# The last of three chained products as seven half-size block products per pair of token tiles

## The chip, the cores and the metric

One core of one Trainium2 chip runs the whole program. The metric is the device time of one execution in microseconds (us). TensorE (PE) multiplies, VectorE (DVE) and ScalarE (ACT) do the elementwise work, GpSimd (POOL) small steps, and the SyncE queue (SP) issues the transfers, DMA transposes among them.

## The reference, cut to what matters

```python
def _attn_ref(q, k, v, g_norm):                     # 4 batches, 8 heads, 576 tokens, 64 wide
    kv = np.einsum('bhsd,bhse->bhde', k, v)
    out = np.einsum('bhsd,bhde->bhse', q, kv)
    rms = np.sqrt(np.mean(out * out, axis=-1, keepdims=True) + 1e-06)
    return out / rms * g_norm                       # -> x: 2304 tokens x 512

def _moe_ref(x, w_in, w_out):                       # 512 -> 2048 -> 512
    h = x @ w_in
    sp = np.where(h > 20.0, h, np.log1p(np.exp(np.minimum(h, 20.0))))
    return (h * np.tanh(sp)) @ w_out

def _moe2_ref(x, w_in, w_out, g_ln):                # 512 -> 1024 -> 512
    h = x @ w_in
    e = np.exp(h - np.max(h, axis=-1, keepdims=True))
    solu = h * (e / (np.sum(e, axis=-1, keepdims=True) + 1e-09))
    mu = np.mean(solu, axis=-1, keepdims=True)
    var = np.mean((solu - mu) ** 2, axis=-1, keepdims=True)
    return ((solu - mu) / np.sqrt(var + 1e-06) * g_ln) @ w_out     # the last product
```

The weights arrive as 64-bit floats.

## The kernel before, in words

**Number form.** A value that goes into a large product is kept as two fp16 parts, a high one (a rounding, by ACT) and a low one (the rest, by DVE), and a product of two such values is three matmuls (`PASS`: high*high, high*low, low*high), added up in PSUM.

**First mixture.** The 2304 tokens are six blocks of 384 (b = 0 to 5), the 2048 hidden columns four groups of 512 (g). PE runs 24 units H(b, g) (lines 595 to 606: four times 12 matmuls of 384 columns) and 24 units Y(b, g) (lines 631 to 646: the same number), H ahead of Y, so that the Y units of the last block are over last. `w1` and `w2` hold the weights of the two products, `g` (three buffers) the activations between them. The staging tiles `st` (five) and `P` (five) serve to decode the weights: ACT scales (`sc`), POOL takes signs (`sg`), DVE joins the bits (`low`, `put`), ACT makes the high part (`whi`), DVE the low one (`wlo`). The pieces of the second mixture's weights, `w3` (8) and `w4` (8), go the same way, late in the first mixture, into a pool of their own (`w34`).

**Second mixture.** It goes by 18 token tiles t of 128. H2(t) (lines 709 to 726) is 24 matmuls of 512 columns into one of two two-bank PSUM tiles. Then comes the row work: the row's maximum on DVE (`mx`), the exponential on ACT (`ex`), the product `z` on DVE, its sum of squares on ACT (`sq2`), small steps on DVE and POOL (`inv`, `var`, `pw`), the normalisation on DVE (`ln`), the high part on ACT (`hi`), the low part on DVE (`lo`), one DMA transpose from `hl` into `lnT` (`T`, line 790). O(t) (lines 794 to 805) is 24 matmuls of 512 columns into one PSUM bank: 8 slices of the 1024 inputs, times three passes, 128 tokens by all 512 output columns. ACT scales the bank into `osb` (`oc`, line 809) and SP writes it out (`out`, line 812). H2(t) needs `z` of tile t-2, since that frees its PSUM tile.

**Order.** The program first collects tasks with an engine, a cost, what they come after and, for PE, a due time from a nominal sequence (`pe`, lines 222 to 226, and `nominal`). A list planner (`Plan.order`) then lays them out per engine: at each engine the one that is ready and due first. `Plan.search` moves due times of tasks of the first 160 us at random, 300 times, and keeps what does not lengthen the plan's end. What comes out is one fixed order per engine; at run time each engine goes through its queue and waits on semaphores. Where the plan leaves PE a gap in the first 150 us, `keep_warm` (line 1066) puts idle matmuls of 256 columns there.

Of the kernel before, what the change touches and what calls it, by code (L numbers as in the profile page):

```python
# [8 lines left out]
FP32 = mybir.dt.float32  # L9
# [131 lines left out]
def tile_attn_moe_moe2(  # L141
# [52 lines left out]
    psA = psA_cm.__enter__()  # L194


    st_p = ctx.enter_context(pool("stage", NST, side="right"))
    dec_p = ctx.enter_context(pool("dec", NDEC, side="right"))
    g_p = ctx.enter_context(pool("g", NG, side="right"))
# [21 lines left out]
    hs, ys = iter(units), iter(units)  # L221
    pe = [("H", *next(hs)) if x == "H" else ("Y", *next(ys)) for x in line]
    pe += [("2", 0), ("2", 1)] + [("Y", *u) for u in ys] + [("2", 2)]
    for t in range(3, NT2):
        pe += [("O", t - 3), ("2", t)] if t < NT2 - 1 else [("2", t)]
    pe += [("O", t) for t in range(NT2 - 4, NT2)]
    MM = 0.1625
    nominal, at_ = {}, 26.0
    for u in pe:
        nominal[u] = at_  # L230
        at_ += 48 * MM if u[0] in "HY" else 24 * 0.216

# [258 lines left out]
    W_in, W_out, W2_in, W2_out = (words(x) for x in (w_in, w_out, w2_in, w2_out))  # L491

    def w1_item(f):
        s = slice(f * 128, (f + 1) * 128)
# [22 lines left out]
    def w4_item(kk):  # L517
        def load(t):
            nc.sync.dma_start(out=t, in_=W2_out[kk * 128:(kk + 1) * 128, :])
        return (load, (lambda: (w34["w4"][:, kk, 0], w34["w4"][:, kk, 1])),  # L520
                gl[:, kk:kk + 1], 1)
# [5 lines left out]
    PIECES += [("3", j) for j in range(8)] + [("4", j) for j in range(8)]  # L527
    ITEM = {"1": w1_item, "2": w2_item, "3": w3_item, "4": w4_item}
    items = {u: ITEM[u[0]](u[1]) for u in PIECES}
    piece = {}  # L530

    def w_load(u):
        t = st_p.tile([128, 1024], I32, tag="st", name="st")
        items[u][0](t)
        piece[u] = [t, None]

# [69 lines left out]

# [7 lines left out]

    def g_hi(b, grp, i):
        if i == 0:
            g_t[b, grp] = g_p.tile([128, 2, G, BLK], FP16, tag="g", name="g")
# [66 lines left out]
    def open_w34():  # L684
        at_cm.__exit__(None, None, None)
        w34_cm.append(pool("w34", 1, side="right"))
        p = w34_cm[0].__enter__()
        w34["w3"] = p.tile([128, C, 2, F2], FP16, name="w3")
        w34["w4"] = p.tile([128, K2, 2, DM], FP16, name="w4")


    ph2 = {}
# [87 lines left out]
    def s_hi(t):  # L780
        hl = T[t, "hl"] = ph2["p"].tile([128, 2, F2], FP16, tag="hl", name="hl")
        nc.scalar.activation(out=hl[:, 0], in_=T[t, "z"], func=ACTF.Copy)  # L782

    def s_lo(t):
        hl = T[t, "hl"]
        nc.vector.tensor_tensor(out=hl[:, 1], in0=T[t, "z"], in1=hl[:, 0], op=ALU.subtract)  # L786

    def s_T(t):
        lnT = T[t, "lnT"] = st_p.tile([128, 2 * K2, 128], FP16, tag="st", name="lnT")
        nc.sync.dma_start_transpose(out=lnT, in_=T[t, "hl"].rearrange("p a f -> p (a f)"))  # L790

    outv = out.rearrange("(b p r) c -> b r p c", p=128, r=R)

    def emit_O(t):
        lnT = T[t, "lnT"]
        w4 = w34["w4"]
        op = T[t, "op"] = psY.tile([128, 512], FP32, tag=f"y{t % 4}", name="op")
        m = 0
        for kk in range(K2):
            for la, wa in PASS:  # L800
                nc.tensor.matmul(  # L801
                    out=op, lhsT=lnT[:, K2 * la + kk], rhs=w4[:, kk, wa],
                    start=(m == 0), stop=(m == 3 * K2 - 1),
                )
                m += 1

    def o_copy(t):
        osb = T[t, "osb"] = dec_p.tile([128, DM], FP32, tag="P", name="osb")
        nc.scalar.activation(out=osb, in_=T[t, "op"], func=ACTF.Copy, scale=2.0 ** -16)

    def o_out(t):
        nc.sync.dma_start(out=outv[t // R, t % R], in_=T[t, "osb"])


    def task(key, engine, cost, fn, args, after=(), lag=0.1, due=None):
# [170 lines left out]
    for n, (b, grp) in enumerate(units):  # L986
# [16 lines left out]
        if last:  # L1003
# [17 lines left out]
                    last_of[c] = [("ylo", b, c)]  # L1021


    task(("open2",), "-", 0.0, open_2, (),
         [("glo", *u, i) for u in units for i in range(2)]
         + [("ylo", b, c) for b in range(NI) for c in range(C)] + [("open",)], 0.0)
    for t in range(NT2):
        y = [("ylo", t // R, c) for c in range(C)]
        w = [("wlo", ("3", j)) for j in range(8)]
        task(("2", t), "P", 5.2, emit_H2, (t,),  # L1030
             [("open2",)] + y + w + ([("z", t - 2), ("2", t - 1)] if t > 1 else []), 0.25,
             nominal["2", t])
# [11 lines left out]
        stb = ("put", PIECES[len(PIECES) - NST + t]) if t < NST else ("O", t - NST)  # L1044
        task(("T", t), "S", 1.4, s_T, (t,), [("lo", t), stb], 2.6)
        w = [("wlo", ("4", j)) for j in range(8)]
        bank = last_of[t] if t < 4 else [("oc", t - 4)]
        task(("O", t), "P", 5.2, emit_O, (t,),
             [("T", t), ("O", t - 1) if t else None] + w + bank, 0.25, nominal["O", t])
        decb = ("wlo", PIECES[len(PIECES) - NDEC + t]) if t < NDEC else ("out", t - NDEC)  # L1050
        task(("oc", t), "A", 0.58, o_copy, (t,), [("O", t), decb])
        task(("out", t), "S", 0.9, o_out, (t,), [("oc", t)], LAND)


    nc.scalar.preload_act_table_set("mish")
# [83 lines left out]
```

## Time and profile before

| what | value |
|---|---|
| median of 3 runs | 626.46 us |
| all runs | 626.46, 749.81, 624.45 us |
| span of the profiled execution | 624.8 us |
| PE busy share of the span | 99% |
| matmuls of the last product | 432 of 512 columns |

The span runs from the first to the last instruction of the one profiled execution. It lies between the two lower runs and 1.7 us below the median. Busy time of PE is not PE at its peak, since matmuls overlap; what one matmul costs in a stream is the distance from start to start.

### The profile page before, as it was taken

The page shows a single profiled execution, that of the slowest core. Times are in us where ns is not written, and L with a number is a line of the kernel's source. Part 1 is how long each engine was busy: PE and PEld are TensorE (multiplying, and loading weights), DVE is VectorE, ACT ScalarE, POOL GpSimd, SP SyncE. Part 2 cuts the span into 40 slices and gives each one's busy share as a digit, 9 for nine tenths or more (in the row PEclk, how much of TensorE's full clock was granted, in tenths as well). Part 3 has the DMA queues.
Part 4 walks back from the last instruction along what each step waited for, and adds up shares of the span by engine and source line. Part 5 has one row for each costly group of instructions (what it writes and reads, how often), then busy time and mean ns, then how long its engine had stood idle before and what let it go on. Part 6 is the DMA issues. An engine that isn't in the chain of part 4 may idle for free.

```text
span 624.8 us, 9988 instructions
## 1 busy us (share of the span) xinstructions
PE 616.5 (99%) x4103; PEld 353.7 (57%) x4103; DVE 310.9 (50%) x534; ACT 267.3 (43%) x459; POOL 95.5 (15%) x126
## 2 busy tenths in 40 slices
PE   8999999999999999999999999999999999999997
PEld 6766666666666666566666666654445444444443
DVE  1688788882113531333122288937777245555410
ACT  3668557663313423332333266616444233343311
POOL 1534632210000210013001143200010000000000
PEclk9899999999999999999999999999999999999999
DMA  8999685852022250014000254201430533343331
GB/s 295 300 255 209 186 175 169 268 99 64 1 77 77 57 121 1 0 35 69 17 2 18 76 211 169 102 1 34 69 67 5 120 78 76 76 79 74 80 106 50
DMA packets 97965, 61.99 MB, mean 99 GB/s; under 512 B 72064, under 2 KB 89472, under 8 KB 97920
## 3 DMA queue, kind: packets, MB, share of 16 engines
q1 hardware_dynamic: 97760, 61.36, 38.7%
q8 instruction: 32, 0.52, 0.4%
q14 instruction: 13, 0.11, 0.1%
q10 hardware_dynamic: 160, 0.00, 0.0%
HBM read 39.33 MB, written 4.72 MB: 70 GB/s over the span
## 4 chain that ended last, share of the span: by engine, by line
PE 92%; DMA 5%; ACT 2%; SPq 0%; DVE 0%; issue 0%; ACTq 0%
PE y L641 30%; PE hp L601 28%; PE op L801 15%; PE h L718 15%; DMA qraw<-in_q_dram 2%; DMA st<-in_moe_w_in_dram 2%; PE kvp L294 2%; PE xo L432 1%; DMA xT<-xhl 1%; DMA yT<-in_k_dram 1%; ACT P L542 0%; PE rT L370 0%; ACT qhl L406 0%; ACT xhl L468 0%; ACT g L618 0%; ACT m L611 0%
## 5 line engine op out<-in xcount | busy, mean ns | idle before, releaser
L641 PE MATMUL y<-g,w 128*128 128x384 f16 x1152 | 201.3, 326 | 0.0
L601 PE MATMUL hp<-xT,w 128*128 128x384 f16 x960 | 166.7, 327 | 0.8 <-DMA xT<-xhl 0.5
L601 PEld LDWEIGHTS <-w 128*128 128x128 f16 x1152 | 111.8, 98 | 75.2 <-issue 1.3
L641 PEld LDWEIGHTS <-w 128*128 128x128 f16 x1152 | 111.8, 98 | 74.4
L718 PE MATMUL h<-w,yT 128*128 128x512 f16 x432 | 96.0, 379 | 0.0
L801 PE MATMUL op<-w,lnT 128*128 128x512 f16 x432 | 95.2, 379 | 0.0
L623 DVE SCALAR_TENSOR_TENSOR g<-m,g 128x768 f16<-128x768 f32 x48 | 46.3, 970 | 95.6 <-ACT g L618 95.5
L611 ACT ACTIVATE m<-hp 128x384 f32<-128x384 f32 x96 | 46.2, 488 | 107.3 <-PE hp L601 106.4
L801 PEld LDWEIGHTS <-lnT 128*128 128x128 f16 x432 | 42.3, 98 | 50.7
L718 PEld LDWEIGHTS <-yT 128*128 128x128 f16 x432 | 42.3, 98 | 50.1
L547 POOL TENSOR_SCALAR st<-st 128x512 f32<-128x512 f32 x48 | 43.6, 918 | 101.5 <-ACT P L542 98.0
L618 ACT ACTIVATE g<-m 128x768 f16<-128x768 f32 x48 | 39.9, 838 | 26.2 <-PE y L641 25.7
L552 DVE SCALAR_TENSOR_TENSOR st<-st 128x512 int32<-128x512 int32 x48 | 36.6, 780 | 11.2 <-POOL st L547 11.2
L735 ACT ACTIVATE e<-h,nb 128x1024 f32<-128x1024 f32 x18 | 20.1, 1116 | 51.4 <-DVE nb L730 30.2
L542 ACT ACTIVATE P<-st 128x512 f32<-128x512 f32 x48 | 31.7, 669 | 15.8 <-DMA st<-in_moe_w_out_dram 7.9
L452 POOL TENSOR_SCALAR ms<-ms 128x8 f32<-128x8 f32 x15 | 5.4, 363 | 210.4 <-DVE ms L447 210.1
L559 DVE SCALAR_TENSOR_TENSOR P<-P,st 128x512 int32<-128x512 int32 x48 | 34.5, 745 | 0.1
L601 PE MATMUL hp<-yT,w 128*128 128x384 f16 x192 | 33.3, 326 | 0.0
L729 DVE TENSOR_REDUCE mx<-h 128x1 f32<-128x1024 f32 x18 | 22.0, 1224 | 20.5 <-PE h L718 20.5
L768 POOL TENSOR_SCALAR var<-var 128x1 f32<-128x1 f32 x18 | 3.4, 190 | 178.9 <-DVE var L763 178.9
L742 DVE SCALAR_TENSOR_TENSOR z<-h,e 128x1024 f32<-128x1024 f32 x18 | 22.0, 1224 | 17.5 <-ACT e L735 17.5
L786 DVE TENSOR_TENSOR hl<-z,hl 128x1024 f16<-128x1024 f32 x18 | 22.0, 1224 | 14.9 <-ACT hl L782 14.9
(95 smaller groups left out, 438.8 us busy)
## 6 DMA issues: line engine op xcount, KB each, us to landing
st<-in_moe_w_in_dram SPq DMA_DIRECT2D x24, 512.0 KB, 5.4
st<-in_moe_w_out_dram SPq DMA_DIRECT2D x24, 512.0 KB, 4.4
yT<-in_k_dram SPq DMA_DIRECT2D x16, 288.0 KB, 5.4
yT<-in_v_dram SPq DMA_DIRECT2D x16, 288.0 KB, 5.6
out_dram<-osb SPq DMA_DIRECT2D x18, 256.0 KB, 2.8
qraw<-in_q_dram SPq DMA_DIRECT2D x3, 768.0 KB, 6.3
qraw<-in_q_dram SPq DMA_DIRECT2D x4, 384.0 KB, 8.2
qraw<-in_q_dram SPq DMA_DIRECT2D x4, 192.0 KB, 5.2
```

The source lines that it names most:

```text
L542: nc.scalar.activation(out=P, in_=v[:, :, 1], func=ACTF.Copy, scale=2.0 ** -111)
L547: nc.gpsimd.tensor_scalar(out=v[:, :, 1], in0=v[:, :, 1], scalar1=0.0, scalar2=1.0, op0=ALU.mult, op1=ALU.mult)
L552: nc.vector.scalar_tensor_tensor(out=v[:, :, 0], in0=v[:, :, 0], scalar=29, in1=v[:, :, 1], op0=ALU.logical_shift_right, op1=ALU.bitwise_or)
L559: nc.vector.scalar_tensor_tensor(out=P.bitcast(I32), in0=P.bitcast(I32), scalar=3, in1=v[:, :, 0], op0=ALU.logical_shift_left, op1=ALU.bit ...
L601: nc.tensor.matmul(out=h_t[b, grp, i], lhsT=w1[:, c, wa, f:f + 128], rhs=xT_t[b][:, C * xa + c], start=(c == 0 and m == 0), stop=(c == C - ...
L611: nc.scalar.activation(out=m_t[b, grp, i // 2][:, i % 2], in_=h_t.pop((b, grp, i)), func=ACTF.Mish, scale=2.0 ** -16)
L618: nc.scalar.activation(out=g_t[b, grp][:, 0, 2 * i:2 * i + 2], in_=m_t[b, grp, i], func=ACTF.Copy, scale=64.0)
L623: nc.vector.scalar_tensor_tensor(out=g_t[b, grp][:, 1, j], in0=m_t.pop((b, grp, i)), scalar=64.0, in1=g_t[b, grp][:, 0, j], op0=ALU.mult, ...
L641: nc.tensor.matmul(out=y_t[cc][:, 0:BLK], lhsT=w2[:, grp * G + ii, wa, cc * 128:(cc + 1) * 128], rhs=g_t[b, grp][:, ga, ii], start=(first ...
L718: nc.tensor.matmul(out=hp[:, half], lhsT=y[:, c, ya, tok], rhs=w3[:, c, wa, half * 512:(half + 1) * 512], start=(m == 0), stop=(m == 3 * C ...
L729: nc.vector.reduce_max(out=mx, in_=T[t, "hp"], axis=AX.X)
L801: nc.tensor.matmul(out=op, lhsT=lnT[:, K2 * la + kk], rhs=w4[:, kk, wa], start=(m == 0), stop=(m == 3 * K2 - 1),)
```

## The change

The tiles are taken in nine pairs. The pair's 256 rows of normalised `z` are a 2x2 block matrix, tile by half of the 1024 inputs, and the weight `w4` is a 2x2 block matrix, half of the inputs by half of the 512 output columns. O(p) for pair p is seven block products in Strassen's manner (Winograd's sums), each 4 slices x 3 passes = 12 matmuls of 256 columns, in the order 1, 2, 6, 7, 5, 4, 3. They need four sums of row blocks per pair (`s_sum`) and four sums of weight blocks, once (`w4_sums`). Products 6, 5, 3 go on top of product 1 in one PSUM bank (A), product 4 on top of 7 in another (D), product 2 stands alone (B). Between the additions intermediate states are taken out: `e1` (after 1), `e2` (after 6) and `e7` (after 7) by ACT into `part_e`, `c11`, `c22`, `c21` by DVE and `c12` by ACT into the output rows.

Places: the seven weight blocks lie in the first 14 of 16 column blocks of `w1` (whose layout is now by column block), the transposed rows (two buffers) in `w2`, `part_e` in the ends of both, and the rows before the transpose (`HL`, two buffers) over all the staging tiles `st` and over all of `g`. So these wait for the last reads of what lay there.

```diff
-    w1 = big.tile([128, C, 2, F1], FP16, name="w1")
+    w1 = big.tile([128, F1 // 128, C, 2, 128], FP16, name="w1")
...
-    for t in range(3, NT2):
-        pe += [("O", t - 3), ("2", t)] if t < NT2 - 1 else [("2", t)]
-    pe += [("O", t) for t in range(NT2 - 4, NT2)]
+    pe += [("2", 3)]
+    for p in range(2, NT2 // 2):
+        pe += [("2", 2 * p), ("2", 2 * p + 1), ("O", p - 2)]
+    pe += [("O", p) for p in range(NT2 // 2 - 2, NT2 // 2)]
...
+    w4 = w1f[:, 0:56 * HB].rearrange("p (k a q n) -> p k a q n", k=4, a=2, q=7)
+    lnTs = [w2f[:, 7168 * i:7168 * i + 7168].rearrange("p (c t) -> p c t", t=128) for i in range(2)]
...
+    def w4_scale(u):
+        P = piece[u][1]
+        nc.scalar.activation(out=P, in_=P, func=ACTF.Copy, scale=items[u][2])
+    def w4_sums(j):
+        a, b, t = piece["4", j][1], piece["4", j + 4][1], w34["t4"]
+        lo, hi = slice(0, HB), slice(HB, 2 * HB)
+        for o, x, y in ((t[:, 0], a[:, hi], a[:, lo]), (t[:, 1], b[:, hi], t[:, 0]),
+                        (t[:, 2], b[:, hi], a[:, hi]), (t[:, 3], b[:, lo], t[:, 1])):
+            nc.vector.tensor_tensor(out=o, in0=x, in1=y, op=ALU.subtract)
...
+    HL = [st_all.rearrange("p n w -> p (n w)").bitcast(FP16), g_all.rearrange("p n a i t -> p (n a i t)")]
+    SUMS = ((4, 2, 3, ALU.add), (5, 4, 0, ALU.subtract), (6, 0, 2, ALU.subtract),
+            (7, 1, 5, ALU.subtract))
+    PART = {"a": (0, 2, 0), "b": (3, 6, 2), "c": (6, 8, 5)}
+    def s_sum(p):
+        Q = T[p, "Q"]
+        for o, x, y, op in SUMS:
+            nc.vector.tensor_tensor(out=Q[:, o], in0=Q[:, x], in1=Q[:, y], op=op)
...
+    PROD = {1: (0, 0, "A", True), 2: (1, 1, "B", True), 6: (4, 4, "A", False),
+            7: (5, 5, "D", True), 5: (3, 3, "A", False), 4: (2, 6, "D", False),
+            3: (6, 2, "A", False)}
+    ORDER = (1, 2, 6, 7, 5, 4, 3)
+    def emit_O(p, i):
+        x, w, bank, first = PROD[i]
...
+        for kk in range(4):
             for la, wa in PASS:
                 nc.tensor.matmul(
-                    out=op, lhsT=lnT[:, K2 * la + kk], rhs=w4[:, kk, wa],
+                    out=T[p, bank][:, 0:HB], lhsT=lnTs[p % 2][:, 8 * x + 4 * la + kk],
+                    rhs=w4[:, kk, wa, w], start=(first and m == 0),
...
-        task(("hi", t), "A", 1.05, s_hi, (t,), [("ln", t)] + ([("T", t - 2)] if t > 1 else []))
-        task(("lo", t), "V", 1.23, s_lo, (t,), [("hi", t)])
-        task(("T", t), "S", 1.4, s_T, (t,), [("lo", t), stb], 2.6)
-        task(("oc", t), "A", 0.58, o_copy, (t,), [("O", t), decb])
...
+        if p > 1:
+            before = [("T", p - 2, x) for x in "abc"]
+        elif p:
+            before = [("Yd", *u) for u in units[-NG:]]
+        else:
+            before = [("put", u) for u in PIECES[-NST:]]
+        task(("sum", p), "V", 2.8, s_sum, (p,), lns)
...
+        for x, c in (("a", 1.4), ("b", 2.1), ("c", 1.4)):
+            buf = [("O", p - 2, i) for i in ORDER] if p > 1 else [("Yd", *u) for u in (units[-4:] if p else units[-4:-2])]
+            task(("T", p, x), "S", c, s_T, (p, x), [("lo", p, x)] + buf, 2.6)
+        where = {1: "a", 2: "a", 6: "b", 7: "c", 5: "b", 4: "b", 3: "c"}
+            needs = {6: [("e1", p)], 5: [("e2", p)], 4: [("e7", p)], 3: [("c22", p)]}.get(i, [])
...
+        task(("e1", p), "A", 0.38, o_keep, (p, 0, "A"), [("O", p, 1)] + old + gate)
+        task(("e2", p), "A", 0.38, o_keep, (p, 1, "A"), [("O", p, 6)] + old + gate)
+        task(("e7", p), "A", 0.38, o_keep, (p, 2, "D"), [("O", p, 7)] + old + gate)
+        task(("c11", p), "V", 0.42, o_add, (p, 0, 0, "B", 0), [("O", p, 2), ("e1", p)] + slots + decb)
+        task(("c22", p), "V", 0.42, o_add, (p, 1, 1, "A", 2), [("O", p, 5), ("e7", p)] + slots + decb)
+        task(("c21", p), "V", 0.42, o_add, (p, 1, 0, "D", 1), [("O", p, 4), ("e2", p), ("c22", p)])
+        task(("c12", p), "A", 0.38, o_copy, (p,), [("O", p, 3), ("c11", p)])
```

Part "a" of a pair is its first tile (two blocks), "b" three blocks (the second tile's second half and two sums), "c" the other two sums; each has its own `hi`, `lo` and transpose. The pair's `z` blocks and sums lie in `Q`, two buffers. The weight part for slice j (`w4t`, `w4hr`, `w4ht`, `w4lr`, `w4lt`) waits for the units H(5, ·) that read the column blocks of `w1` that it overwrites.

## Rows read from the trace of the kernel before

**Rows 1.** The page: busy time by engine, granted clock in 40 slices, the chain by engine and line
```profile
PE 616.5 (99%) x4103; PEld 353.7 (57%) x4103; DVE 310.9 (50%) x534; ACT 267.3 (43%) x459; POOL 95.5 (15%) x126
PEclk9899999999999999999999999999999999999999
PE 92%; DMA 5%; ACT 2%; SPq 0%; DVE 0%; issue 0%; ACTq 0%
```

**Rows 2.** Windows (start:end, length; busy us and count per engine; clock, DMA share, GB/s)
```profile
0.00:60.00 60.00, 55.35 (x671) 40.47 (x671) 36.57 (x69) 36.35 (x70) 22.80 (x31) 0.97 1.01 264
360.00:420.50 60.50, 60.50 (x366) 35.62 (x364) 44.97 (x60) 33.54 (x59) 15.76 (x16) 1.00 0.34 120
420.50:585.00 164.50, 164.50 (x793) 77.50 (x792) 94.42 (x208) 67.56 (x101) 12.59 (x34) 1.00 0.34 69
440.00:480.00 40.00, 40.00 (x205) 19.83 (x203) 31.11 (x69) 19.05 (x30) 3.69 (x10) 1.00 0.29 51
564.28:585.00 20.72, 20.72 (x98) 9.41 (x96) 11.04 (x24) 7.97 (x12) 1.48 (x4) 1.00 0.35 77
585.00:624.80 39.80, 36.26 (x169) 16.23 (x166) 5.52 (x12) 7.57 (x12) 0.74 (x2) 1.00 0.27 73
```

**Rows 3.** Timeline of PE and weight loads (start us, length, line, shape, count, idle before)
```profile
47.35 3.33 PE L1068 MATMUL hp<-ident 128*128 128x256 f16 x29
47.35 3.04 PEld L1068 LDWEIGHTS <-ident 128*128 128x128 f16 x28
...
409.27 2.11 PE L601 MATMUL hp<-xT,w 128*128 128x384 f16 x12
...
489.65 2.11 PE L641 MATMUL y<-g,w 128*128 128x384 f16 x12
...
574.48 5.34 PE L801 MATMUL op<-w,lnT 128*128 128x512 f16 x24
...
584.84 36.42 PE L801 MATMUL op<-w,lnT 128*128 128x512 f16 x168
```

**Rows 4.** Groups by shape (count; busy us, mean ns of one), second mixture
```profile
L801 PEld LDWEIGHTS <-lnT 128*128 128x128 f16 x432 | 42.3, 98 | 50.7
L786 DVE TENSOR_TENSOR hl<-z,hl 128x1024 f16<-128x1024 f32 x18 | 22.0, 1224 | 14.9 <-ACT hl L782 14.9
L782 ACT ACTIVATE hl<-z 128x1024 f16<-128x1024 f32 x18 | 19.0, 1053 | 21.5 <-DVE z L777 17.6 <-DMA lnT<-hl 3.8
L809 ACT ACTIVATE osb<-op 128x512 f32<-128x512 f32 x18 | 10.6, 588 | 30.6 <-PE op L801 30.5
```

**Rows 5.** Groups by shape up to 420 us: nearest forms to the new instructions
```profile
L459 DVE SCALAR_TENSOR_TENSOR xf<-xo,rho 128x512 f32<-128x512 f32 x15 | 10.4, 691 | 19.9 <-POOL rho L454 19.9
L579 DVE SCALAR_TENSOR_TENSOR w<-P,gl,w 128x512 f16<-128x512 f32 x8 | 5.6, 741 | 0.1
L677 DVE SCALAR_TENSOR_TENSOR yT<-y,yT 128x384 f16<-128x384 f32 x8 | 4.5, 556 | 11.9 <-ACT yT L669 11.8
L311 DVE SCALAR_TENSOR_TENSOR kvr<-kvp,kvr 64x256 f16<-64x256 f32 x6 | 2.5, 419 | 0.3 <-ACT kvr L305 0.2
L611 ACT ACTIVATE m<-hp 128x384 f32<-128x384 f32 x96 | 46.2, 488 | 107.3 <-PE hp L601 106.4 <-DVE g L623 0.6
```

**Rows 6.** Transfers of the second mixture: size, count, us from issue to landing
```profile
out_dram<-osb SPq DMA_DIRECT2D x18, 256.0 KB, 2.8
lnT<-hl SPq DMA_TRANSPOSE x18, 4.3
```

**Rows 7.** Timeline: first row maximum, the last tile's transpose issue, first and last output copies
```profile
420.50 1.23 DVE L729 TENSOR_REDUCE mx<-h 128x1 f32<-128x1024 f32 x1 [6.73 <-PE h L718]
...
590.22 0.60 ACT L809 ACTIVATE osb<-op 128x512 f32<-128x512 f32 x1 [2.44 <-PE op L801]
...
596.61 1.83 SPq L790 DMA_TRANSPOSE lnT<-hl  x1
...
621.35 0.60 ACT L809 ACTIVATE osb<-op 128x512 f32<-128x512 f32 x1 [4.58 <-PE op L801]
```

More of the change, by code (lines that the diff above doesn't have):

```diff
@@ L194, in tile_attn_moe_moe2 @@
     psA = psA_cm.__enter__()
-    st_p = ctx.enter_context(pool("stage", NST, side="right"))
+    st_p = ctx.enter_context(pool("stage", 1, side="right"))
+    st_all = st_p.tile([128, NST, 1024], I32, name="st")
     dec_p = ctx.enter_context(pool("dec", NDEC, side="right"))
-    g_p = ctx.enter_context(pool("g", NG, side="right"))
+    g_p = ctx.enter_context(pool("g", 1, side="right"))
+    g_all = g_p.tile([128, NG, 2, G, BLK], FP16, name="g")
     at_cm = pool("attn", 1, side="right")
@@ L519, in load @@
             nc.sync.dma_start(out=t, in_=W2_out[kk * 128:(kk + 1) * 128, :])
-        return (load, (lambda: (w34["w4"][:, kk, 0], w34["w4"][:, kk, 1])),
-                gl[:, kk:kk + 1], 1)
+        return load, None, gl[:, kk:kk + 1], 1
     w34 = {}
@@ L616, in g_hi @@
         if i == 0:
-            g_t[b, grp] = g_p.tile([128, 2, G, BLK], FP16, tag="g", name="g")
+            g_t[b, grp] = g_all[:, units.index((b, grp)) % NG]
         nc.scalar.activation(
@@ L792, in tile_attn_moe_moe2 @@
-    outv = out.rearrange("(b p r) c -> b r p c", p=128, r=R)
[L794 to L797, printed above, removed]
+    HL = [st_all.rearrange("p n w -> p (n w)").bitcast(FP16), g_all.rearrange("p n a i t -> p (n a i t)")]
+    HL = [x[:, 0:14 * 512].rearrange("p (q a f) -> p q a f", q=7, a=2) for x in HL]
+    SUMS = ((4, 2, 3, ALU.add), (5, 4, 0, ALU.subtract), (6, 0, 2, ALU.subtract),
+            (7, 1, 5, ALU.subtract))
@@ L798, in emit_O @@
+    ORDER = (1, 2, 6, 7, 5, 4, 3)
+    def emit_O(p, i):
+        x, w, bank, first = PROD[i]
+        if first:
+            n = (3 * p + "ABD".index(bank)) % 4
+            T[p, bank] = psY.tile([128, 512], FP32, tag=f"y{n}", name="op")
         m = 0
-        for kk in range(K2):
+        for kk in range(4):
             for la, wa in PASS:
                 nc.tensor.matmul(
-                    out=op, lhsT=lnT[:, K2 * la + kk], rhs=w4[:, kk, wa],
-                    start=(m == 0), stop=(m == 3 * K2 - 1),
+                    out=T[p, bank][:, 0:HB], lhsT=lnTs[p % 2][:, 8 * x + 4 * la + kk],
+                    rhs=w4[:, kk, wa, w], start=(first and m == 0),
+                    stop=(m == 11), skip_group_check=not first,
@@ L804, in emit_O, with o_keep @@
                 )
                 m += 1
[L807 to L812, printed above, removed]
+    OUT = 2.0 ** -16
+    def o_keep(p, n, bank):
+        e = T[p, "e", n] = part_e[p % 2][:, n]
+        nc.scalar.activation(out=e, in_=T[p, bank][:, 0:HB], func=ACTF.Copy, scale=OUT)
@@ new lines, in osb, with o_add, o_copy @@
+    def osb(p, t):
+        if (p, "osb", t) not in T:
+            T[p, "osb", t] = dec_p.tile([128, DM], FP32, tag="P", name="osb")
+        return T[p, "osb", t]
+    def o_add(p, t, half, bank, n):
+        nc.vector.scalar_tensor_tensor(
+            out=osb(p, t)[:, half * HB:half * HB + HB], in0=T[p, bank][:, 0:HB], scalar=OUT,
+            in1=T[p, "e", n], op0=ALU.mult, op1=ALU.add)
+    def o_copy(p):
+        nc.scalar.activation(
+            out=osb(p, 0)[:, HB:2 * HB], in_=T[p, "A"][:, 0:HB], func=ACTF.Copy, scale=OUT)
@@ L1050, in tile_attn_moe_moe2 @@
-        decb = ("wlo", PIECES[len(PIECES) - NDEC + t]) if t < NDEC else ("out", t - NDEC)
-        task(("oc", t), "A", 0.58, o_copy, (t,), [("O", t), decb])
-        task(("out", t), "S", 0.9, o_out, (t,), [("oc", t)], LAND)
+    for p in range(NT2 // 2):
+        if p > 1:
[4 more added lines that the diff above has]
+            before = [("put", u) for u in PIECES[-NST:]]
+        lns = [("ln", 2 * p), ("ln", 2 * p + 1)]
+        task(("hi", p, "a"), "A", 1.05, s_hi, (p, "a"), lns[:1] + before)
+        task(("lo", p, "a"), "V", 1.23, s_lo, (p, "a"), [("hi", p, "a")])
+        task(("sum", p), "V", 2.8, s_sum, (p,), lns)
+        for x, c in (("b", 1.45), ("c", 1.05)):
+            task(("hi", p, x), "A", c, s_hi, (p, x), [("sum", p)] + before)
+            task(("lo", p, x), "V", c + 0.2, s_lo, (p, x), [("hi", p, x)])
+        for x, c in (("a", 1.4), ("b", 2.1), ("c", 1.4)):
+            buf = [("O", p - 2, i) for i in ORDER] if p > 1 else [("Yd", *u) for u in (units[-4:] if p else units[-4:-2])]
+            task(("T", p, x), "S", c, s_T, (p, x), [("lo", p, x)] + buf, 2.6)
+        w = [("wlo", ("4", j)) for j in range(4)]
+        where = {1: "a", 2: "a", 6: "b", 7: "c", 5: "b", 4: "b", 3: "c"}
+        bank = {i: (3 * p + n) % 4 for i, n in ((1, 0), (2, 1), (7, 2))}
+        prev = ("O", p - 1, 3) if p else None
+        for i in ORDER:
+            needs = {6: [("e1", p)], 5: [("e2", p)], 4: [("e7", p)], 3: [("c22", p)]}.get(i, [])
+            if i in bank:
+                n = bank[i]
+                needs = list(free_y.get(n, last_of[n])) if p else list(last_of[n])
+            task(("O", p, i), "P", 1.32, emit_O, (p, i), [("T", p, where[i])] + w + needs,
+                 0.25, nominal["O", p] + 1.32 * ORDER.index(i))
+            if prev:
+                plan.line([prev, ("O", p, i)])
+            prev = ("O", p, i)
+        old = [("c11", p - 2), ("c22", p - 2), ("c21", p - 2)] if p > 1 else []
+        gate = [("H", NB - 1, 3, i) for i in range(G)] if p == 0 else [("Yd", *units[-1])] if p == 1 else []
+        decb = ([("wlo", u) for u in PIECES[-NDEC:]] if p < 3 else [])
+        slots = [("out", p - 2, 0), ("out", p - 2, 1)] if p > 1 else []
+        task(("e1", p), "A", 0.38, o_keep, (p, 0, "A"), [("O", p, 1)] + old + gate)
[5 more added lines that the diff above has]
+        task(("c12", p), "A", 0.38, o_copy, (p,), [("O", p, 3), ("c11", p)])
+        task(("out", p, 0), "S", 0.9, o_out, (p, 0), [("c11", p), ("c12", p)], LAND)
+        task(("out", p, 1), "S", 0.9, o_out, (p, 1), [("c21", p), ("c22", p)], LAND)
+        free_y[(3 * p) % 4] = [("c12", p)]
+        free_y[(3 * p + 1) % 4] = [("c11", p)]
+        free_y[(3 * p + 2) % 4] = [("c21", p)]
```

91 lines of the change are left out of this document (66 added, 25 removed).

## The prediction

> **What bounds it now.** I read the page first: PE is busy for 99% of the span, the chain that ended last is PE for 92%, and the granted clock stands at 9 tenths of full speed or more in all but the second of the 40 slices [rows 1], that is at the upper of its two levels. So a microsecond comes off only where PE issues fewer or shorter matmuls, and anything that makes PE wait is added in full. The windows say where PE did idle: 4.65 us in the first 60 us, and after its last matmul; from 360 us to 585 us it was busy throughout [rows 2]. DVE has most to do of the others: 74% of 360 to 420.5 us, 57% of 420.5 to 585 us, 78% of 440 to 480 us, where units of Y lay between the H2 tiles (the last 12 matmuls of Y begin at 489.65) [rows 2, 3]. PE still idled nowhere there, so 78% is a DVE load that this order is known to bear. The timeline gives the price of a matmul in a stream, from start to start: 168 of 512 columns in 36.42 us make (36.42 - 0.379)/167 = 0.2158 us each, 12 of 384 columns (2.11 - 0.326)/11 = 0.162 [rows 3].
>
> **The last product.** Removed: per pair 48 matmuls of 512 columns, 48 x 0.2158 = 10.36 us. Added: 7 x 12 = 84 of 256 columns. None such is in the last product before, but the idle matmuls of `keep_warm` have just this shape, each with a weight load: 29 in 3.33 us, (3.33 - 0.273)/28 = 0.1092 us [rows 3]; a straight line through 384 and 512 columns gives 0.1086. I take 0.1092: 84 x 0.1092 = 9.17 us. The gain is 1.19 us per pair, 10.7 us for nine (11.1 at 0.1086). That is 1.7%, and no other term of PE shrinks, so 624.8 - 10.7 = 614.1 us is the floor but for what the search may find in the first 60 us.
>
> Weight loads rise from 432 to 756, 98 ns each [rows 4], and now sit under matmuls of 109 ns. The idle stream shows 28 such loads in the same 3.33 us [rows 3], so they are hidden, with 11 ns to spare. The Trainium skill (TensorE: Matmul & The Clock Gate, section on packing small matmuls, The mechanism) says that a weight load overlaps matmuls in flight only where their row groups differ, which speaks against this change: all 128 rows are used here, and a pair would cost 84 x (0.109 + 0.098) = 17.4 us by it. The trace does not bear that out, at 256 columns or at 384.
>
> **Waits within a product.** Product 6 waits for `e1`, 5 for `e2`, 4 for `e7` (ACT), 3 for `c22` (DVE); between what they wait for and them lies one other product, 12 x 0.1092 = 1.31 us. An ACT copy of 256 columns out of PSUM is 0.39 us (from 488 ns at 384 and 588 at 512), a DVE addition 0.42 (419 for 64x256; 556 at 384 is its upper end) [rows 4, 5]; the chain moves from PE to the output copy within 0.1 us (the first of the seven tiles ends about 590.2, the copy starts at 590.22) [rows 3, 7]. That leaves 0.85 us. Behind `e1` on ACT are queued the exponentials and squares, behind `c22` the maxima and `z`; PE waits if the engine stands in something longer, or in something that is itself late. On DVE those are the maxima and `lo` at 1.22 (4 per pair), the three-block `lo` at 1.76, and the four sums, 4 x 0.69 = 2.76 if together. At a random moment this costs ((1.22 - 0.85)^2/2 x 4 + 0.91^2/2 + 1.91^2/2)/19.53 = 0.13 us for `c22`; the ACT waits a tenth of it each. That is 1.5 us over nine pairs. The order is fixed in advance and every lag shifts it, so I take 4 us, 0.11 us for each of the 36 waits; the ends are 0 and 18 (0.5 us each).
>
> **DVE and ACT.** A pair of tiles now takes DVE 11.04 us of 20.72 [rows 2]. The change adds the sums (2.76; 691 ns each from a DVE instruction of two inputs and 512 columns [rows 5]), a `lo` of 1536 columns (1.224 + 512 x 1.044 ns = 1.76; the slope is from 556 at 384 to 1224 at 1024 [rows 4, 5]) beside the two of 1024 that stay, and three additions (1.26): 16.82 us. PE needs 2 x 5.18 + 9.17 = 19.53 us, so DVE stands at 86%. ACT goes from 7.97 to 7.97 - 1.18 + 1.45 + 1.56 = 9.80 us, 50%. DVE stays below PE, and H2 can run well ahead of O (two buffers each of `Q`, `HL` and `lnT`), so its lag is bridged, until the last pair. Over the stage DVE has 94.42 + 5.52 us [rows 2] plus 9 x 5.78 = 152 us. It starts at 420.5 [rows 7]; its last `lo` must be over when the transpose (4.3 us [rows 6]) and the last four products (5.24 us) still fit before PE's end, 621.3 - 10.7 = 610.6: by 601. That is 152 of 180.5 us, 84%.
>
> **Weights.** `w4` costs DVE 8 x 0.741 = 5.9 us now [rows 5]. After: 16 subtractions of 256 columns (6.7) and low parts 4 x (0.42 + 0.69 + 1.22) = 9.3, so 10.1 us more; ACT has 8 x 0.59 + 4 x (0.39 + 0.59 + 1.05) = 12.8 where about 8 x 0.59 = 4.7 were, 8 more. In 360 to 420.5 us DVE goes from 45.0 to 55.1 of 60.5 us, ACT from 33.5 to 42 [rows 2]. The cover is the 6.73 us in which DVE waits for the first maximum [rows 7] and the last three units of Y, 3 x 48 x 0.162 = 23 us of PE, that come before O(0). I cost it at nothing; without the cover up to 10 us go into the DVE stage above, which then needs 90%. The waits for old places (`w1`, `w2`, `st`, `g`) end with H(5, ·), the last `put` and the last Y. The strictest is pair 1, whose rows lie over `g` and wait for all of Y; while they wait PE has Y itself and H2. Nothing.
>
> **Transposes.** Three per pair where there were two, with 1.75 times the columns, on SP's queue, each behind O of two pairs before. A DMA share of 0.35 [rows 2] becomes at most 0.61. Hidden, but at the end. There the last transpose was issued 11.6 us after the last H2 (585.0 to 596.61 [rows 2, 7]); the sums and the longer `hi` and `lo` add 2.76 + 0.4 + 0.54, and the landing takes 4.3 to 6.5 us (three blocks for two), so product 6 of the last pair can start 19.6 to 21.8 us after the last H2. If two pairs and two products are left for PE then, that is 2 x 9.17 + 2.62 = 20.96 us of work. Before, seven tiles were left (36.42 us [rows 3]), so I expect three pairs or more, and charge 1 us; with one pair left it would be 9.
>
> **The sum.** 624.8 - 10.7 + 4 + 1 = 619.1. The span lies between the shown runs, 1.7 us below their median; I say 619.
>
> **Rivals.** About 2% is what a measurement of this kernel can tell from no change, so between 613.9 and 639 us (612.3 and 637.3 on the scale of the span) it is called the same.
>
> First, the waits within a product take the gain. At 10.7/36 = 0.30 us for each of the 36 the gain is gone (624.8), at (637.3 - 614.1)/36 = 0.64 it is over 2% slower; at 0.5 it gives 614.1 + 18 = 632. For it: a DVE at 86% and a fixed order; PE has no other ready work when H2 in turn waits for `z`. Against: 0.85 us of slack at each, and ACT half idle.
>
> Second, the one on the other side: DVE becomes the bound, in the stage after 420.5 us. The 180.5 us above grow by as much as the end is late, so it decides from where DVE can be kept busy for no more than 79% of the time (152/(180.5 + 10.7): no gain) and 75% (152/(180.5 + 23.2): over 2% slower). With 80% and 5 us of weights left over, 157/0.8 = 196 us, 15.7 late: 630. For it: nothing in the trace shows more than 78% in this stage. Against: that was what was asked of it, not its limit; with H2 ahead there is nearly always another tile's step ready.
>
> Third, it doesn't do what it says: 256 columns cost more than 0.1092 us in this stream, where operands and weights change at every matmul, unlike in the idle one. At 10.36/84 = 0.1233 the gain is gone; with loads wholly exposed, 756 x 0.098 = 74 us more, 688. The skill's rule above would give that. The hidden loads at 384 and 256 columns speak against it: a chance of 0.03, 0.01 of it for the loads wholly exposed.
>
> Fourth, over 2% faster: nearly no waits, and up to 4.65 us of PE's idle time in the first 60 us [rows 2] gone, as the search runs anew and keeps other moves. 609.5 at best. It can as well lose some.
>
> **Chances.** Forecast 0.68 (its own range 614 to 624), waits 0.13, DVE 0.11, matmul price 0.03, faster 0.05. Over 2% slower: a third of the waits' case, under a half of DVE's, most of the third: 0.12. Faster 0.05, the rest 0.83. The range leaves out the faster case and the upper halves of the first two rivals with the third, under 0.2: 613 to 632.
>
> **What would show it.** Right: products of 12 matmuls 1.31 us apart, PE without gaps over 0.2 us in O, DVE at 80 to 90% from 430 to 590 us, three or more pairs after the last H2. Wrong: PE idle before products 6, 5, 4 released by ACT, or before 3 by DVE (first rival); PE idle before H2, released by `z`, or one long gap in the last pair behind a transpose (second); a stream of 256 columns over 0.115 us (third); idle time before 415 us that was not there, if the weights' cover fails.

## The result, and the profile after

The changed kernel takes 617.5 us (616.5 to 618.0) where the kernel before takes 625.66 us: a ratio of 0.9873, interval 0.9857 to 0.989. One of the four runs behind the 625.66 was slow (749.81 us); the ratio is that of the fast runs. Forecast were 619 us and 613 to 632. The profiled execution has a span of 614.5 us and a time of 616.5 us; before, the span was 624.8 us.

The page of the changed kernel, the same parts as in [rows 1]:

```profile
PE 602.5 (98%) x4427; PEld 382.7 (62%) x4427; DVE 365.0 (59%) x626; ACT 289.5 (47%) x498; POOL 95.9 (16%) x126
PEclk9999999999999999999999999999999999999999
PE 90%; DMA 6%; ACT 2%; issue 1%; DVE 1%; POOL 0%; SPq 0%; POOLq 0%; ACTq 0%
```

PE is still what the time hangs on: it lost 14 us of busy time, while DVE gained 54 and ACT 22.

PE's timeline (start us, length, shape, count, idle time before and what ended it). L861 is the last product, L753 is H2, L676 is Y:

```profile
474.93 2.11 PE L676 MATMUL y<-g,w 128*128 128x384 f16 x12
476.88 5.40 PE L861 MATMUL op<-w,w 128*128 128x256 f16 x48
482.67 5.40 PE L861 MATMUL op<-w,w 128*128 128x256 f16 x48 [0.39 <-DVE osb L880]
489.12 5.41 PE L861 MATMUL op<-w,w 128*128 128x256 f16 x48 [1.04 <-DMA w<-g]
494.37 5.34 PE L753 MATMUL h<-w,yT 128*128 128x512 f16 x24
499.55 1.47 PE L861 MATMUL op<-w,w 128*128 128x256 f16 x12
500.86 5.34 PE L753 MATMUL h<-w,yT 128*128 128x512 f16 x24
506.04 8.02 PE L861 MATMUL op<-w,w 128*128 128x256 f16 x72
...
582.85 17.19 PE L861 MATMUL op<-w,w 128*128 128x256 f16 x156
600.43 10.64 PE L861 MATMUL op<-w,w 128*128 128x256 f16 x96 [0.39 <-DVE osb L880]
```

Three things are to be seen. The price: 156 matmuls of 256 columns in 17.19 us are (17.19 - 0.273)/155 = 0.1091 us each. The waits: there are three. From start to start, 476.88 + 48 x 0.1092 = 482.12 to 482.67 is 0.55 us, to 489.12 it is 1.21, to 600.43 it is 0.54: together 2.3 us. (In brackets the profile gives the idle time alone, which is some 0.16 us less for each.) And the order: the planner put H2 between product 1 of a pair and the other six (12, then 24 of H2, then 72), and three pairs were left after the last H2 (156 + 96 matmuls).

Windows, columns as in [rows 2]: the first 60 us, the time in which the weights are made ready, three pairs in the middle, and the stage from the first row maximum on:

```profile
0.00:60.00 60.00, 53.27 (x682) 38.91 (x683) 38.47 (x72) 38.03 (x73) 23.25 (x31) 1.00 1.01 273
360.00:420.50 60.50, 60.50 (x367) 35.67 (x365) 52.48 (x79) 39.62 (x69) 14.32 (x15) 1.00 0.31 108
500.86:559.45 58.59, 58.59 (x399) 38.75 (x397) 46.32 (x96) 28.66 (x45) 4.43 (x12) 1.00 0.62 127
420.50:614.50 194.00, 188.75 (x1273) 124.17 (x1271) 145.45 (x292) 89.41 (x140) 14.23 (x36) 1.00 0.55 110
```

A pair takes 58.59/3 = 19.53 us of PE, the forecast figure, and DVE is busy for 79% of it, where 86% were forecast.

The balance of the spans: 624.8 - 10.7 + 2.3 = 616.4. The other 1.9 us lie ahead of the change, in the first 60 us. The first unit of Y, behind the same sequence of matmuls, begins 1.77 us earlier in the changed kernel (the second line is that of the kernel before), and from there to the second mixture PE does not idle in either:

```profile
60.26 2.11 PE L676 MATMUL y<-g,w 128*128 128x384 f16 x12
62.03 2.11 PE L641 MATMUL y<-g,w 128*128 128x384 f16 x12
```

The granted clock of the first 60 us was 1.00 here and 0.97 before [rows 2].

### The profile page after: what moved, and what is told of

Read it like the earlier page. It is cut to its first block, busy times and chain, and to the rows that moved or that the text cites. A ratio compares the mean times of both kernels' runs of the same rounds, so it can differ in the third digit from the quotient of the medians.

```text
span 614.5 us, 10823 instructions
## 1 busy us (share of the span) xinstructions
PE 602.5 (98%) x4427; PEld 382.7 (62%) x4427; DVE 365.0 (59%) x626; ACT 289.5 (47%) x498; POOL 95.9 (16%) x126
## 4 chain that ended last, share of the span: by engine, by line
PE 90%; DMA 6%; ACT 2%; issue 1%; DVE 1%; POOL 0%; SPq 0%; POOLq 0%; ACTq 0%
PE y L676 31%; PE hp L636 29%; PE h L753 15%; PE op L861 12%; DMA st<-in_moe_w_in_dram 3%; PE kvp L297 2%; PE xo L435 1%; DMA w<-g 1%; DMA qraw<-in_q_dram 1%; DMA xT<-xhl 1%; DMA yT<-in_k_dram 1%; ACT P L542 0%; POOL rho L457 0%; PE rT L373 0%; ACT m L646 0%
## 5 line engine op out<-in xcount | busy, mean ns | idle before, releaser
L676 PE MATMUL y<-g,w 128*128 128x384 f16 x1152 | 201.2, 326 | 0.0
L636 PEld LDWEIGHTS <-w 128*128 128x128 f16 x1152 | 111.9, 98 | 74.3 <-issue 1.2
L676 PEld LDWEIGHTS <-w 128*128 128x128 f16 x1152 | 111.8, 98 | 73.9
L753 PE MATMUL h<-w,yT 128*128 128x512 f16 x432 | 96.0, 379 | 0.0
L861 PE MATMUL op<-w,w 128*128 128x256 f16 x756 | 85.2, 273 | 1.8 <-DMA w<-g 1.0
L861 PEld LDWEIGHTS <-w 128*128 128x128 f16 x756 | 73.8, 98 | 13.5 <-DMA w<-g 1.3
L753 PEld LDWEIGHTS <-yT 128*128 128x128 f16 x432 | 42.3, 98 | 48.0
L542 ACT ACTIVATE P<-st 128x512 f32<-128x512 f32 x48 | 32.0, 673 | 19.3 <-DMA st<-in_moe_w_in_dram 12.2
L786 ACT ACTIVATE e<-Q,nmz 128x1024 f32<-128x1024 f32 x18 | 20.7, 1148 | 20.6 <-DVE nmz L782 20.5
L779 DVE SCALAR_TENSOR_TENSOR Q<-h,e 128x1024 f32<-128x1024 f32 x18 | 21.9, 1219 | 6.5 <-ACT e L770 6.5
```

Of the source, the lines that this page charges most:

```text
L542: nc.scalar.activation(out=P, in_=v[:, :, 1], func=ACTF.Copy, scale=2.0 ** -111)
L636: nc.tensor.matmul(out=h_t[b, grp, i], lhsT=w1[:, f, c, wa], rhs=xT_t[b][:, C * xa + c], start=(c == 0 and m == 0), stop=(c == C - 1 and m ...
L676: nc.tensor.matmul(out=y_t[cc][:, 0:BLK], lhsT=w2[:, grp * G + ii, wa, cc * 128:(cc + 1) * 128], rhs=g_t[b, grp][:, ga, ii], start=(first ...
L753: nc.tensor.matmul(out=hp[:, half], lhsT=y[:, c, ya, tok], rhs=w3[:, c, wa, half * 512:(half + 1) * 512], start=(m == 0), stop=(m == 3 * C ...
L861: nc.tensor.matmul(out=T[p, bank][:, 0:HB], lhsT=lnTs[p % 2][:, 8 * x + 4 * la + kk], rhs=w4[:, kk, wa, w], start=(first and m == 0), stop ...
```

## The experiments

In none of them is a part of the computation left out; what is repeated gives the same values again. Those up to e7 leave the costs in the plan alone, so that every engine's order is that of the changed kernel (in e4, that of the kernel before).

**e1, an eighth product.** PE gets 12 matmuls per pair back.

```diff
+        for again in range(2 if i == 2 else 1):
             m = 0
             for kk in range(4):
...
```

> The changed kernel with product 2 of every pair computed twice, in the same place and with the same fixed order on every engine: 12 matmuls of 256 columns more per pair, 96 in place of 84. If the time is set by the columns that PE issues, it goes up by 9 x 12 x 0.1092 = 11.8 us, from 617.5 to 628 to 630, back to or above the kernel before. If DVE or the waits within a product set the end, PE's extra work falls into time in which it waits anyway, and the time goes up by less than 3 us.

628.1 us, ratio to before 1.0033 (1.0021 to 1.0046). That is 10.6 us more than the changed kernel, for 11.8 us of matmuls; PE's waits after 405 us, by releaser, shrank to one line, the transpose wait being filled:

```profile
PE op L861 <- DMA w<-g: 1.0, 1, 1.0
PE op L861 <- DVE osb L880: 0.8, 2, 0.4
PE op L862 <- DVE osb L881: 0.8, 2, 0.4
```

The first two lines are the changed kernel's, the third is e1's. The transpose's wait is 1.2 us from start to start, and 11.8 - 1.2 = 10.6: the time follows PE's columns, as far as medians tell. With all of the change's other work kept, the gain goes with PE's 84 matmuls in place of 96; there is no sign of another source.

**e4, the kernel before in halves.** Half-size matmuls without Strassen's sums.

```diff
-        for kk in range(K2):
+        for half in range(2):
+            s = slice(256 * half, 256 * half + 256)
...
-                    out=op, lhsT=lnT[:, K2 * la + kk], rhs=w4[:, kk, wa],
+                        out=op[:, s], lhsT=lnT[:, K2 * la + kk], rhs=w4[:, kk, wa, s],
```

> The kernel before with its last product in two halves of 256 columns per token tile: 864 matmuls of 256 columns where there were 432 of 512, the same sums, the same results, twice the weight loads. If a matmul of 256 columns costs 0.1092 us with its weight load hidden, a pair takes 96 x 0.1092 = 10.48 in place of 10.36 us: 1.1 us in all, about 626.5. If the price were 0.1233 us, 13 us more (638); with the loads exposed 85 us more (710).

626.91 against 625.54 us in the same runs, 1.0019 (1.0002 to 1.0036): 1.4 us for an expected 1.1. Its last seven tiles (compare [rows 3]):

```profile
585.78 36.84 PE L803 MATMUL op<-w,lnT 128*128 128x256 f16 x336
```

(36.84 - 0.273)/335 = 0.1092 us, with a weight load for each. The third rival falls.

**e3 and e6, the copies two and four times.** How much room the product between leaves for a wait.

```diff
+        for _ in range(2):
             nc.scalar.activation(out=e, in_=T[p, bank][:, 0:HB], func=ACTF.Copy, scale=OUT)
```

> The changed kernel with each of the three copies of intermediate states out of PSUM (ACT, 0.38 us) done twice, the order unchanged. If the product that lies between covers the wait with 0.85 us to spare, as predicted, nothing changes (617 to 619). If these waits are what PE's time hangs on, each of the 27 copies adds its 0.38 us: about 628.

> The changed kernel with each copy of an intermediate state done four times: 1.52 us where the product between takes 1.31, the order unchanged. Doing it twice cost nothing. If the product between is the cover, two or three products per pair now come 0.2 to 0.4 us late: 0.5 to 0.8 us per pair, 622 to 625. If the copies are covered by more than that product (H2 between the products), nothing: 617 to 619. If each copy were on PE's path, 27 x 1.14 = 31 us: 648.

Twice: 617.35 us, 0.9861 (0.9836 to 0.9886) where the changed kernel has 0.9873: nothing. No product waited for a copy. But the two waits for an addition doubled in the trace (first line below; 0.4 us each in the changed kernel), while the transpose's fell from 1.0 to 0.6, so a copy that is longer does reach PE where another engine stands behind it. Four times: 628.31 us, 1.0037 (1.0023 to 1.005), 10.8 us more, beyond the 4.5 to 7.5 that I expected. The waits of e6 after 405 us (second and third line), and one pair of its timeline:

```profile
PE op L861 <- DVE osb L881: 1.6, 2, 0.8
PE op L861 <- ACT w L873: 7.5, 15, 1.0
PE op L861 <- DVE osb L881: 2.1, 2, 1.1
...
508.20 4.09 PE L861 MATMUL op<-w,w 128*128 128x256 f16 x36
...
511.04 3.15 ACT L873 ACTIVATE w<-op 128x256 f32<-128x256 f32 x8
512.71 4.31 PE L861 MATMUL op<-w,w 128*128 128x256 f16 x36 [0.42 <-ACT w L873]
```

Products 2, 6 and 7 run on; `e2` and `e7` are now one train of eight copies from 511.04 to 514.19, product 5 starts 0.58 us late (508.20 + 36 x 0.1092 = 512.13 to 512.71) and the next three take 4.31 in place of 4.09: 0.8 us, the upper end of what was expected. That holds for the pairs in the middle, where H2 stands behind product 1. For the pairs at either end there is no H2 left to put there, product 6 comes late too, and `c22` behind it: with 0.8 us for each of four pairs in the middle, those five cost (10.8 - 3.2)/5 = 1.5 us each. So the room in front of the products that wait for a copy is between 0.38 us, which none of them felt, and 1.14 us, which they did: the 0.85 us of the prediction lie between.

**e5 and e2, more work on DVE.** Two, then all four row sums computed twice.

```diff
-        for o, x, y, op in SUMS:
+        for o, x, y, op in SUMS * 2:          # e2; e5: SUMS + SUMS[:2]
```

> The changed kernel with two of the four row sums computed twice: 1.37 us of DVE more per pair, half of what e2 added, 12.4 us in all, the order unchanged. e2 (24.8 us more DVE work) cost 12.4 us. If DVE has a reserve of some 12 us and only what goes beyond it is paid, this costs 0 to 2 us (617.5 to 620). If the cost is in proportion, because every microsecond of DVE delays something in the fixed order, it costs 6 us (623 to 624).

> The changed kernel with the four sums of row blocks computed twice per pair: DVE has 4 x 0.687 = 2.75 us more per pair, 19.6 us where PE has 19.5, the order of all engines unchanged. If DVE has the room that the prediction gave it (152 us needed of 180), 177 us still fit, and the time stays within 5 us (617 to 622). If DVE can't be kept busy for more than about 85% of the time, its last low part comes 177/0.85 - 180 = 28 us late, and the time is about 645.

e5: 622.1 us, 0.9939 (0.9918 to 0.996), 4.6 us more for 12.4 us of DVE work. e2: 629.89 us, 1.0064 (1.0043 to 1.0086), 12.4 us more for 24.8. (Sums in a row overlap a little: DVE's busy time rose by 10.7 and 21.6 us.) Neither theory of e2 was right, and of e5 the second came near: there is no free reserve of 12 us, nor is the work paid in full. Who kept PE waiting in e2:

```profile
PE op L861 <- DVE yT L712: 4.3, 1, 4.3
PE op L861 <- ACT w L872: 4.0, 6, 1.7
PE op L861 <- DMA w<-g: 1.1, 1, 1.1
PE op L861 <- DMA w<-st: 1.0, 2, 0.8
PE op L861 <- DVE osb L880: 0.6, 2, 0.4
PE h L753 <- DVE Q L779: 0.3, 1, 0.3
```

The waits are spread over every kind of thing that DVE, or ACT behind DVE, hands to PE; only the last line is H2 held up by `z`.

**e8 and e11, the same load with an order made for it.** e8 tells the planner of the doubled sums; e11 also makes each sum a task of its own and takes e9's landing time.

```diff
-        task(("sum", p), "V", 2.8, s_sum, (p,), lns)
+        task(("sum", p), "V", 5.55, s_sum, (p,), lns)                          # e8
...
+        for n, a in enumerate((lns, [("sum", p, 0)], lns, [("sum", p, 1)])):   # e11
+            task(("sum", p, n), "V", 1.38, s_sum, (p, n), a)
```

> e2 again (the four row sums twice), but with the planner told of it: their cost is 5.55 in place of 2.8, so the order on every engine is made for it. e2 gave 629.9. If it was DVE's capacity that set the end there, a better order changes little: 628 to 631. If it was the order, made for shorter sums, most of the 12.4 us come back: 618 to 623. Both parts: in between.

> The four row sums computed twice once more (24.8 us more of DVE in all), now with the best order known: each sum a task of its own that the planner may put other work between, told of its doubled cost, and with the landing of transposes as in e9. e9 without the doubled sums gave 614.3, e8 (told, one block) 625.8. If the 11.5 us between them were DVE's capacity, it stays at 624 to 627. If they were the block of sums in front of an addition that PE waits for, PE's waits at the end go and it comes to 614 to 618. As DVE then has 19.6 us per pair where PE has 19.5, I expect part of both: 619 to 622.

e8: 625.8 us, 0.9996 (0.9982 to 1.001), so 4.1 of e2's 12.4 us were the order. What is left is in one place, near the end; the first line is a window ahead of it (columns as in [rows 2]), in which PE never waits although DVE is busy for 89%:

```profile
480.00:580.00 100.00, 100.00 (x690) 67.42 (x689) 89.17 (x180) 46.57 (x76) 8.06 (x20) 1.00 0.69 135
...
592.67 5.14 DVE L826 TENSOR_TENSOR Q<-Q 128x512 f32<-128x512 f32 x8
592.80 1.47 PE L861 MATMUL op<-w,w 128*128 128x256 f16 x12 [3.16 <-DVE osb L880]
599.33 21.05 PE L861 MATMUL op<-w,w 128*128 128x256 f16 x168 [5.06 <-DVE osb L880]
```

Product 3 of a pair waits for an addition that runs at 592.33, behind other row work, and the product after it for one that runs at 598.86, behind the eight sums and a low part. A part of the 8.3 us is not waiting: the 168 matmuls behind the longer wait took 21.05 us, where the price above gives 0.273 + 167 x 0.1092 = 18.5, with the granted clock down to 0.75 from 599 to 610 us. In e11 the sums are split, but it came to 623.33 us, 0.9963 (0.9948 to 0.9977), 9 us more than e9, which has the order without the load, and slower than the 619 to 622 that I expected. PE's waits there:

```profile
PE op L862 <- DMA w<-g: 4.1, 3, 2.6
PE op L862 <- DVE osb L881: 2.5, 1, 2.5
PE op L862 <- DMA w<-st: 1.1, 1, 1.1
```

The transposes of the second pair (from `g`) and of the last (from `st`) now come late, and one addition still does. So the order gives back a part, and 8 to 9 of the 24.8 us are paid in both orders that were made for the load. Whether another order would pay less is not shown: in e8 DVE was busy for 19.3 of the 20 us from 580 to 600, so that its sheer load is a second reading there.

**e7, the weight sums three times.** Whether the time that makes the weights ready is really covered.

```diff
-        for o, x, y in ((t[:, 0], a[:, hi], a[:, lo]), (t[:, 1], b[:, hi], t[:, 0]),
+        for o, x, y in 3 * ((t[:, 0], a[:, hi], a[:, lo]), (t[:, 1], b[:, hi], t[:, 0]),
```

> The changed kernel with the sums of weight blocks computed three times: 32 subtractions of 256 columns more, 32 x 0.42 = 13.5 us of DVE between about 365 and 420 us, the order unchanged. If DVE's idle time there and its reserve of some 12 us later are the cover, it costs 0 to 3 us (617 to 621), and the first row maxima come some us later. If the weights stand in front of what PE needs (the first H2, the last Y), PE idles before 425 us and the time goes up by 5 to 13 us (623 to 631).

625.88 us, 0.9996 (0.9981 to 1.0011): 8.4 us more for 13.5. In the changed kernel the weights are ready 2.25 us ahead of the first row maximum (where 6.73 us were idle before [rows 7]); in e7 that maximum comes 7.6 us later, counted from the start of the first H2 (415.27 and 416.74 us), and the third H2 waits for `z`:

```profile
417.17 1.23 DVE L615 TENSOR_TENSOR w<-t,w 128x1024 f16<-128x1024 f32 x1 [0.18 <-ACT w L611]
420.65 1.23 DVE L764 TENSOR_REDUCE mx<-h 128x1 f32<-128x1024 f32 x1 [2.25 <-PE h L753]
429.69 1.22 DVE L764 TENSOR_REDUCE mx<-h 128x1 f32<-128x1024 f32 x1
...
435.28 5.01 PE L753 MATMUL h<-w,yT 128*128 128x512 f16 x14 [6.07 <-DVE Q L779]
```

(The first two lines are the changed kernel's, the others e7's.) The cover was there, with little to spare.

**e9 and e10, the order alone.** The three waits left by the change, and a version that beats both kernels.

```diff
-            task(("T", p, x), "S", c, s_T, (p, x), [("lo", p, x)] + buf, 2.6)
+            task(("T", p, x), "S", c, s_T, (p, x), [("lo", p, x)] + buf, 3.6)
```

> The changed kernel with one number of the planner changed: a row transpose is taken to land 3.6 us after its issue is over where it was 2.6 (the trace shows 4.4 to 5.2 us from issue to landing). Only the order changes. The wait of 1.2 us for pair 1's transpose should go, since the plan now sees it and puts the last units of Y and the row work otherwise, and with it one or both of the 0.5 us waits for an addition: 615.5 to 617. If PE's waits of 2.3 us in the second mixture come from the chip and not from the order, nothing changes: 617 to 618.

> The changed kernel once more, unaltered, on the same chip as e9, so that the two can be compared: 616.5 to 618.

e9: 614.28 us (614.05 to 615.61), 0.9817 (0.9794 to 0.984); e10, the changed kernel again on the same chip, 617.33 us, 0.9861 (0.9836 to 0.9886). The 3.05 us are more than the 1 to 2 expected. (The 4.4 to 5.2 us that the expectation names are medians; the range was 4.3 to 7.4.) In e9 no wait of PE is left after 415 us, and the busy time of PE fills the stage:

```profile
420.50:600.00 179.50, 179.50 (x1197) 117.00 (x1196) 143.37 (x287) 87.30 (x136) 13.62 (x36) 1.00 0.59 110
```

So 2.3 of the 3.05 us are the waits, and they came from the order, not from the chip. The other 0.75 us lie in the first 60 us of the two profiled executions, which are also the medians: their first unit of Y begins at 60.32 us in e9 and at 61.10 in e10. The first profile of the changed kernel, where it begins at 60.26, is longer than e9's by 2.2 us (614.5 and 612.3). So the new order is worth 2.3 us, and not 3.

## Why the prediction held, point by point

**The last product.** Forecast 0.1092 us for a matmul and 10.7 us in all, from idle matmuls of the same shape. Measured 0.1091, and 0.1092 in e4; e1 shows that the gain goes with it. The Trainium skill's sentence on weight loads (TensorE: Matmul & The Clock Gate, section on packing small matmuls, The mechanism) is not borne out here either: 756 loads of 98 ns lie under matmuls 109 ns apart.

**The waits within a product.** Forecast 4 us, 0.11 us for each of 36. Measured 1.1 us, in two of them, both `c22` on DVE; no product waited for a copy by ACT, even when e3 doubled the copies. The mechanism of the two is the one forecast: `c22` could run from about 481.0 us, when product 5 was over, and DVE had just taken up a `lo` of 1.23 us, which itself had waited for its `hi` on ACT, behind the copies:

```profile
481.06 1.23 DVE L836 TENSOR_TENSOR g<-Q,g 128x1024 f16<-128x1024 f32 x1 [2.64 <-ACT g L830]
482.20 0.42 DVE L880 SCALAR_TENSOR_TENSOR osb<-op,w 128x256 f32<-128x256 f32 x1
581.14 27.77 PE L861 MATMUL op<-w,w 128*128 128x256 f16 x252
```

The other wait, at 600.43, has the same form, and in e3 `hi`, `lo` and `c22` all came later. So 4 us was too dear: in this order the bad meeting came twice in 36 times. In the pairs in the middle H2 stands between products 1 and 6 and covers `e1` by 5 us, but nothing shows that this saved a wait: the last line above is from e9, where three pairs run without H2 among them and without a wait. For longer copies it does count: in e6 the same delay costs about twice as much where H2 has run out.

**DVE and ACT.** The groups of the changed kernel beside the durations that were worked out (0.69 for a sum, 1.76 for the long low part, 0.42 for an addition, 0.39 for a copy):

```profile
L826 DVE TENSOR_TENSOR Q<-Q 128x512 f32<-128x512 f32 x36 | 23.3, 687 | 0.6
L836 DVE TENSOR_TENSOR st<-Q,st 128x1536 f16<-128x1536 f32 x5 | 8.8, 1756 | 0.0
L880 DVE SCALAR_TENSOR_TENSOR osb<-op,w 128x256 f32<-128x256 f32 x27 | 11.3, 422 | 12.6 <-PE op L861 8.2 <-ACT w L872 3.9
L872 ACT ACTIVATE w<-op 128x256 f32<-128x256 f32 x27 | 10.3, 380 | 24.0 <-PE op L861 24.0
```

Each was right to 3%. The stage took DVE 145.5 us where 152 were forecast, since instructions that follow each other without a wait overlap a little (four sums in 2.62 us, where 4 x 0.687 is 2.75; over the stage the durations add up to 157.4 us). That DVE does not become the bound was right for this load. But the second rival's arithmetic, a capacity with a threshold at 79 and 75% busy, is not how it goes: in the middle of e8 DVE is busy for 89% and PE never waits. e5, e2, e8 and e11 show that the time grows by a third to a half of each microsecond of work that DVE gets more, already with the first 12; in the orders made for the load this is paid at the ends of the stage, in the old order also wherever a short instruction stands behind long ones. In e8, with DVE busy for 158.9 of the 179.5 us from 420.5 to 600, it had cost 8.3 us.

**The weights.** Costed at nothing, rightly; DVE went to 52.5 us in 360 to 420.5, where 55.1 were forecast. The cover named (6.73 us) shrank to 2.25.

**The step that failed** is a later sentence of that part: that pair 1's rows lie over `g` and wait for all of Y was costed at nothing, "while they wait PE has Y itself and H2". The last Y ends at about 477 us, the three transposes from `g` are issued from 476.76 on (the third at 482.75, behind its low part, the 1.23 us shown above, and it lands 6.3 us later), and H2 had run out for the same reason: tile 8's needs `z` of tile 6, whose place pair 1's low parts free (that `z` starts at 483.0 us), and in the fixed order it then stood behind the products. PE did what products it had, and waited 1.21 us for the third transpose. It is the largest of the three waits.

**The transposes at the end.** Forecast 1 us if three pairs or more are left after the last H2. Three were left, and no transpose was late there: 0. The margin was small: the last transpose was issued at 601.2 us and landed 4.4 us later, and the product that reads it begins at 600.43 + 48 x 0.1092 = 605.67.

**The sum.** 4 + 1 us of waits were 2.3, so 616.4 on the span's scale for the forecast 619.1; with the first 60 us of that execution 614.5. In times, 617.5 for 619. The sign "PE without gaps over 0.2 us in O" failed at three places, all told above. And a part of the nearness is luck. The 5 us of waits were put in other places than the 2.3 came from: 1.1 us instead of 4, none instead of 1, and 1.2 where nothing was charged. And the time of an execution lies 2.0 us above its span (616.5 and 614.5), so that a span of 619.1 us would be a time of 621; the prediction called it 619.

## What to carry to other kernels

Where one engine is busy for 99% of the span, count its instructions and take the price of one from the nearest stream in the trace, however unimportant that stream is: the idle matmuls gave the price of the new ones to a tenth of a per cent. What the other engines get in exchange is free only as long as no short instruction that the bound engine waits for stands behind a long one; this depends on the order of the queues and not on the busy share alone, and it fails first where the filler work runs out, at the beginning and at the end of a stage. Where a planner makes that order, its wrong numbers are worth a look: correcting one landing time gave 2.3 us here, beside the 8 of the change itself.

## What the runs showed of the hardware that was not expected

The row transposes took longer to land. From issue to landing, in us (the changed kernel; before, the median was 4.3 [rows 6]):

```profile
DMA to landing us min/median/max: 4.3/4.7/7.4
```

A part of this is size: from 514 to 568 us those of two blocks, as large as the ones before, took 4.3 us and those of three blocks 5.6 or 5.7. Others took longer at the same size where SP's queue held several transfers: pair 1's third, of two blocks and behind two others, took 6.3. The runs do not separate the queue from the transfers that were under way then.

PE's granted clock fell after a long wait: in e7, with 6.07 us idle, it averaged 0.86 over 415 to 440 us (0.50, the lower of its two levels, from 433 to 439 us), where it was 1.00 in the changed kernel, and the 14 matmuls of 512 columns right behind the wait took 5.01 us, where 0.379 + 13 x 0.2158 = 3.18 is their price at 1.00 [rows 3]. So that wait cost 1.8 us more than its length, which makes 7.9 of the 8.4 us. The same shows in e8, by 2.5 us. And the first 60 us differ between executions of the same program: e10's clock there was 0.94, that of the changed kernel's first profile 1.00, with spans of 615.4 and 614.5 us.
